# A two-layer transformer block on one core: idle matrix time filled, loads reordered, and a fixed instruction order taken from a plan

**Chip and metric.** One Trainium2 chip, one of its cores. Times are device microseconds of one execution. Traces and their views are in recorded spans of an execution. Most executions agree within half a per cent.

Names: PE is TensorE (matmul), DVE is VectorE, ACT is ScalarE, POOL is GpSimd, SP is SyncE.

## The reference

The input is one sequence of 2048 rows of 512 in bf16. A dilated local attention (32 heads of 16, every row looks at itself and 7 rows behind it, 2 apart) and a gated ReLU network, each behind a LayerNorm and added to its input:

```python
q, k, v = split(layernorm(x) @ wqkv)            # 512 x 1536
logits  = einsum("bhsd,bhswd->bhsw", q, k[idx]) * scale   # idx = pos - 2*w, w = 0..7, masked below 0
o       = einsum("bhsw,bhswd->bhsd", softmax(logits), v[idx])
h       = x + o @ wo
up, gate = layernorm(h) @ W_up, layernorm(h) @ W_gate     # 512 x 1376
h2      = h + ((gate * (gate > 0)) * up) @ W_down
```

## The kernel before

The rows go in four chunks of 512. Each step (a normalisation, a projection, a score product, a head sum) is an `Op` with an engine, an assumed duration and its inputs. A small planner simulates the engines while the program is built and so decides the order in which each engine gets its instructions; the hardware then runs each engine's list as it stands. `RANK` is a list of one number per operation. In the kernel before it is a priority only: the planner looks at everything that could start now and takes the best rank among it.

```python
LOOK = {"PE": 0.05, "DVE": 0.3, "ACT": 0.1}
def order(self):
    waiting = list(self.ops)
    while waiting:
        best = {}
        for op in waiting:                      # all operations whose inputs are done
            ...                                 # t = when inputs, engine and buffers allow it
            best.setdefault(op.eng, []).append((t, op))
        for eng, cands in best.items():
            first = min(t for t, _ in cands)
            t, op = min(((t, op) for t, op in cands if t <= first + self.LOOK.get(eng, 0.02)),
                        key=lambda x: (x[1].prio, x[1].seq))
        ...
```

What the planner assumes of the loads, and the loads themselves (x of chunk 0, then q, k and v weights, then the other x, then the big weights):

```python
xload = [[load(t) for t in (3.4, 3.5, 3.9, 3.9)]] + [[load(t)] * BPC for t in (9.7, 11.2, 12.7)]
wload = {n: load(t) for n, t in (("q", 6.3), ("k", 7.0), ("v", 8.3), ("o", 14.0), ...)}
...
for c, q in enumerate((nc.sync, nc.scalar, nc.sync)):
    q.dma_start(w3_sb[c][:], w3_r[:, :, c * D:(c + 1) * D])
for tk in range(1, NCK):
    nc.sync.dma_start(x_sm[:, tk * BPC:(tk + 1) * BPC, :], x_rows[:, tk * BPC:(tk + 1) * BPC, :])
```

The normalised rows of chunk 3 are transposed by SP's DMA queue and not by PE, and the first add of a head's eight weighted values is done by an accumulating DMA of POOL for the heads in `DACC`:

```python
DMAT = (("h",2,0),("h",2,2),("x",3,0),("x",3,2))
nc.sync.dma_start_transpose(out=dst.t[:, :, j * P:(j + 1) * P], in_=xn.t[:])
...
DACC = tuple((k, t) for k in range(3) for t in range(4))
nc.gpsimd.dma_start(mt.t[:, 0:4, :], mt.t[:, 4:8, :], accum_op=ALU.add)
```

The softmax here doesn't subtract the row's maximum and nothing guards it: scores larger than these inputs give would overflow.

Of the kernel before, what the change touches and what calls it, by code (L numbers as in the profile page):

```python
# [8 lines left out]
P = 128  # L9
# [8 lines left out]
RANK = [  # L18
    1, 3, 5, 2, 0, 4, 54, 6, 7, 30, 160, 197, 186, 250, 712, 8, 11, 10, 12, 14,
    17, 23, 27, 32, 20, 26, 31, 16, 18, 21, 24, 28, 33, 37, 9, 13, 15, 19, 22, 25,  # L20
    29, 34, 35, 65, 71, 68, 70, 73, 38, 60, 66, 56, 63, 69, 51, 61, 43, 55, 40, 50,
    45, 58, 83, 145, 79, 154, 76, 162, 74, 99, 80, 86, 96, 104, 110, 75, 67, 85, 89, 90,
    171, 179, 185, 114, 136, 123, 133, 128, 94, 113, 101, 108, 118, 148, 159, 183, 189, 193, 156, 170,
    199, 203, 205, 165, 176, 201, 204, 207, 142, 152, 181, 187, 192, 211, 218, 210, 215, 214, 222, 209,
    212, 227, 234, 221, 225, 228, 232, 226, 231, 239, 241, 246, 256, 249, 257, 261, 244, 259, 251, 260,
    264, 292, 321, 277, 317, 267, 313, 324, 333, 340, 280, 305, 270, 304, 301, 308, 303, 310, 315, 295,
    325, 307, 328, 285, 323, 319, 329, 335, 327, 344, 297, 341, 331, 346, 314, 339, 349, 350, 366, 343,
    358, 338, 365, 355, 372, 392, 334, 359, 348, 362, 397, 401, 421, 691, 717, 393, 407, 694, 718, 357,
    420, 701, 721, 363, 423, 699, 720, 39, 47, 44, 48, 36, 41, 42, 46, 49, 52, 62, 78, 64,
    77, 82, 57, 81, 59, 72, 84, 144, 191, 124, 188, 91, 178, 102, 182, 88, 164, 109, 169, 143,  # L30
    172, 117, 168, 147, 252, 139, 300, 87, 299, 151, 302, 195, 174, 224, 245, 229, 208, 238, 248, 253,
    258, 268, 273, 271, 284, 293, 296, 294, 290, 275, 283, 286, 287, 289, 298, 309, 345, 352, 318, 330,
    361, 367, 326, 337, 364, 368, 306, 316, 347, 351, 373, 378, 379, 386, 376, 382, 383, 395, 385, 389,
    391, 396, 390, 394, 398, 400, 402, 403, 406, 413, 408, 415, 419, 411, 417, 412, 418, 422, 431, 456,
    427, 454, 433, 460, 426, 452, 494, 439, 469, 441, 471, 434, 462, 436, 463, 500, 438, 466, 437, 465,
    479, 488, 464, 474, 503, 487, 496, 484, 491, 489, 498, 493, 501, 507, 450, 518, 458, 517, 506, 523,
    499, 520, 526, 447, 508, 444, 509, 524, 516, 536, 709, 726, 510, 530, 707, 725, 522, 538, 705, 723,
    533, 537, 703, 722, 98, 105, 92, 97, 93, 103, 53, 95, 112, 116, 126, 132, 125, 130, 146, 131,
    137, 129, 135, 150, 167, 216, 177, 217, 184, 220, 194, 223, 161, 240, 157, 237, 163, 242, 153, 213,
    173, 428, 175, 409, 202, 416, 219, 356, 236, 254, 265, 312, 274, 263, 288, 320, 322, 332, 336, 342,  # L40
    360, 353, 377, 375, 369, 374, 371, 384, 387, 381, 380, 430, 435, 453, 459, 414, 429, 446, 449, 424,
    432, 451, 457, 399, 425, 443, 448, 467, 473, 461, 468, 475, 482, 470, 478, 477, 480, 472, 476, 485,
    486, 481, 483, 490, 495, 519, 521, 511, 513, 528, 531, 497, 502, 543, 559, 540, 558, 549, 568, 548,
    565, 573, 560, 585, 567, 582, 575, 588, 544, 561, 594, 556, 578, 583, 593, 554, 576, 579, 590, 596,
    552, 570, 563, 580, 546, 564, 553, 574, 591, 616, 625, 572, 618, 599, 621, 608, 623, 631, 620, 630,
    587, 628, 633, 626, 642, 715, 731, 612, 639, 713, 729, 597, 635, 711, 727, 600, 640, 714, 730, 100,
    106, 115, 121, 111, 119, 107, 120, 122, 127, 140, 149, 155, 166, 134, 141, 138, 158, 247, 281, 180,
    255, 196, 269, 190, 266, 243, 279, 235, 278, 200, 272, 230, 276, 233, 541, 198, 505, 262, 550, 206,
    545, 291, 282, 311, 404, 370, 354, 388, 405, 410, 440, 442, 492, 445, 504, 529, 534, 527, 532, 455,
    525, 514, 515, 512, 542, 562, 581, 586, 535, 539, 555, 569, 551, 557, 566, 571, 547, 577, 584, 589,  # L50
    595, 603, 604, 611, 598, 607, 592, 601, 606, 609, 614, 615, 610, 613, 602, 605, 617, 619, 622, 624,
    636, 637, 641, 627, 634, 629, 632, 638, 646, 660, 650, 663, 647, 661, 644, 656, 675, 667, 677, 665,
    674, 673, 681, 670, 678, 684, 659, 671, 654, 668, 657, 669, 662, 672, 682, 651, 664, 652, 666, 643,
    655, 645, 658, 679, 683, 695, 648, 686, 680, 693, 649, 689, 697, 653, 688, 676, 690, 696, 685, 706,
    728, 736, 692, 700, 716, 732, 687, 702, 719, 734, 698, 704, 724, 735, 708, 710, 733, 737,
# [36 lines left out]
class Plan:  # L92
# [21 lines left out]
    GUIDE = ()  # L114

    def order(self):
        for kx, cx, ky, cy in self.GUIDE:
            xs = [o for o in self.ops if o.key and o.key[0].startswith(kx) and o.key[1] == cx]
            for o in self.ops:
                if o.key and o.key[0].startswith(ky) and o.key[1] == cy:  # L120
                    o.deps += xs
        waiting = list(self.ops)
        free = {}
        while waiting:
            best = {}
            for op in waiting:
                t = free.get(op.eng, 0.0)
                ok = True
                for d in op.deps:
                    if d.done is None:  # L130
                        ok = False
                        break
                    r = d.done + (self.HOP if d.eng != op.eng else 0.0)
                    if r > t:
                        t = r
                if not ok:
                    continue
                need = {}
                for b in op.take:
                    if b.i is None:  # L140
                        n = need[b.slots] = need.get(b.slots, 0) + 1
                        r = sorted(b.slots.free)[n - 1]
                        if r == float("inf"):
                            ok = False
                            break
                        t = max(t, r + self.HOP)
                if not ok:
                    continue
                best.setdefault(op.eng, []).append((t, op))
# [10 lines left out]
            t, op = pick  # L160
# [11 lines left out]
            waiting.remove(op)  # L172
# [4 lines left out]
def kernel(  # L177
# [88 lines left out]
    def setup():  # L266
# [4 lines left out]
        for c, q in enumerate((nc.sync, nc.scalar, nc.sync)):  # L271
            q.dma_start(w3_sb[c][:], w3_r[:, :, c * D:(c + 1) * D])
        for tk in range(1, NCK):
            nc.sync.dma_start(x_sm[:, tk * BPC:(tk + 1) * BPC, :], x_rows[:, tk * BPC:(tk + 1) * BPC, :])

        nc.sync.dma_start(wo_sb[:], A_wo.rearrange("(p t) f -> p t f", t=NT))
        nc.sync.dma_start(wu_sb[:], B_W_up.rearrange("(dt p) f -> p dt f", p=P))
        nc.sync.dma_start(wg_sb[:], B_W_gate.rearrange("(dt p) f -> p dt f", p=P))
        nc.sync.dma_start(
            wd_sb[:, 0:NFF, :], B_W_down[0:NFF * P, :].rearrange("(ft p) n -> p ft n", p=P))  # L280
        if FTAIL:
            nc.sync.dma_start(wd_sb[:FTAIL, NFF, :], B_W_down[NFF * P:F, :])

# [10 lines left out]
        nc.gpsimd.memset(vT[:, :, 0:PADL], 0.0)  # L294

# [20 lines left out]
    DACC = tuple((k, t) for k in range(3) for t in range(4))  # L316
    DAL = 5.5
    TDD, TDL = 2.4, 1.6
    NWARM = 48
    DMAT = (("h",2,0),("h",2,2),("x",3,0),("x",3,2))  # L320
# [8 lines left out]

    LNA = ((0, 0, 0, 0), (0, 0, 0, 0))  # L330
# [5 lines left out]
    A5, A10, AX, AS = 0.52, 0.92, 0.8, 0.2  # L336
# [4 lines left out]
    def load(t):  # L341
        return add(None, "LD", 0.0, None, lat=t)

    xload = [[load(t) for t in (3.4, 3.5, 3.9, 3.9)]] + [[load(t)] * BPC for t in (9.7, 11.2, 12.7)]
    wload = {n: load(t) for n, t in
             (("q", 6.3), ("k", 7.0), ("v", 8.3), ("o", 14.0), ("u", 18.0), ("g", 22.0), ("d", 27.0))}

    def layernorm(tk, src, dst_slots, pr, groups, on_act, residual=None):
# [7 lines left out]
        for grp in groups:  # L356
# [3 lines left out]
            for j in grp:  # L360
# [17 lines left out]
                elif tk == 0 and j == BPC - 1:  # L378
# [15 lines left out]
                    a = add(("xsu", tk), "ACT", 0.75, f_su, [src[j]], pr, take=[xns[j], sm], lat=AL)  # L394
                    a = add(("xnm", tk), "DVE", DSM, f_nm, [a], pr, take=[mv], use=[sm], lat=DL)
                    ag.append(add(("xsq", tk), "ACT", 0.75, f_sq, [a], pr, use=[mv, xns[j]], lat=AL))
# [51 lines left out]
            for j0 in range(lo, hi, step):  # L448
# [10 lines left out]
                for j in range(j0, min(j0 + step, hi)):  # L459
# [8 lines left out]
                    ds.append(add((ln + "tp" + gk, tk), "PE", 4 * TP, f_tp, [a], pr, take=[tp], use=[xn], lat=PEL))  # L468
                n = len(ds)
# [15 lines left out]
    wb = Buf(bank_s)  # L485

    def f_warm(wb=wb):
        for _ in range(NWARM):
            nc.tensor.matmul(wb.t[:, 0:P], lhsT=warm[:], rhs=warm[:], start=True, stop=True)

    add(("warm", 0), "PE", 5.2, f_warm, [], -500, take=[wb])

    kdone = {}
    for tk in range(NCK):
# [225 lines left out]
        hnT, hev = layernorm(tk, hd, hnT_s, base + 52, [[0, 1, 2, 3]], LNA[1][tk], residual=sm)  # L720
# [120 lines left out]
```

## Time and profile before

| | before |
|---|---|
| time, median of 3 | 203.58 us (203.55 to 204.13) |
| span of the profiled execution | 203.6 us, its own time 205.38 us |
| busy: PE, DVE, ACT, POOL | 96%, 76%, 63%, 6% |
| mean granted clock of that execution | 0.983 |

The lines of the profile are in the prediction.

### The profile page before, as it was taken

Reading aid. Unit: us, or ns where it says so; the run is one execution under the profiler, and the core shown is the slowest. Engines: PE = TensorE matmul, PEld = TensorE weight load, DVE = VectorE, ACT = ScalarE, POOL = GpSimd, SP = SyncE. Lnnn points to the kernel's source line nnn. Section 1 sums busy time; section 2 is a strip of 40 time slices with the busy share of each in tenths; the row PEclk is TensorE's granted clock in tenths of the full one; section 3 lists DMA queues with packets and bytes.
Section 4 is the critical chain, followed back from the end, with each engine's and each line's share of the span. In section 5 each row is a group of like instructions: output and inputs, shape, how many; then the busy total and the mean of one; then the engine's idle time right before and its main releaser. Section 6 shows DMA issues by size and latency. Waiting matters only on the chain.

```text
span 203.6 us, 2957 instructions
## 1 busy us (share of the span) xinstructions
PE 195.4 (96%) x1102; PEld 96.8 (48%) x1123; DVE 155.1 (76%) x246; ACT 127.7 (63%) x253; POOL 12.6 (6%) x26
## 2 busy tenths in 40 slices
PE   8499999999999999999999999999999999999994
PEld 8347545555545334444454444444444445444452
DVE  6549999999999999999999966599996255021314
ACT  3517879986569993797756599703665353576400
POOL 3000000330000002400033000000000000000000
PEclk9859999999999999999999999999999999999999
DMA  5999901698000002980059900400011001100003
GB/s 187 350 379 403 322 19 30 123 203 163 3 0 0 0 3 52 192 168 0 3 103 180 209 31 0 90 13 0 3 41 62 0 0 53 53 0 0 0 3 103
DMA packets 14893, 18.04 MB, mean 89 GB/s; under 512 B 5056, under 2 KB 12192, under 8 KB 14880
## 3 DMA queue, kind: packets, MB, share of 16 engines
q1 hardware_dynamic: 12336, 10.78, 16.4%
q0 software_dynamic: 1728, 6.29, 16.3%
q10 hardware_dynamic: 816, 0.79, 1.1%
q8 instruction: 9, 0.15, 0.3%
q14 instruction: 4, 0.03, 0.0%
HBM read 8.42 MB, written 2.10 MB: 52 GB/s over the span
## 4 chain that ended last, share of the span: by engine, by line
PE 93%; DMA 4%; issue 1%; SPq 0%; DVE 0%
PE bank L736 38%; PE bank L511 22%; PE bank L773 19%; PE bank L698 7%; DMA wq_sb<-in_A_wqkv_dram 4%; PE bank L564 4%; PE bank L465 2%; PE bank L625 1%; PE bank L597 1%; SPq L270 0%; DVE row L784 0%
## 5 line engine op out<-in xcount | busy, mean ns | idle before, releaser
L736 PE MATMUL bank<-quad,wg_sb 128*128 128x512 bf16 (+1 forms) x171 | 42.3, 379 | 0.3
L736 PE MATMUL bank<-quad,wu_sb 128*128 128x512 bf16 (+1 forms) x173 | 42.3, 379 | 0.1
L743 ACT ACTIVATE gr<-bank 128x512 bf16<-128x512 f32 (+1 forms) x44 | 26.0, 604 | 23.7 <-PE bank L736 18.3
L773 PE MATMUL bank<-wd_sb,gT 128*128 128x512 bf16 (+3 forms) x184 | 39.7, 366 | 0.2
L558 DVE TENSOR_TENSOR big<-quad,kT 128x4096 bf16<-128x4096 bf16 x16 | 36.0, 2284 | 0.1
L646 DVE TENSOR_TENSOR big<-big,vT 128x4096 bf16<-128x4096 bf16 x16 | 35.8, 2283 | 0.3 <-ACT big L631 0.3
L740 ACT CAST up_sb<-bank 128x512 bf16<-128x512 f32 (+1 forms) x44 | 25.7, 594 | 12.3 <-PE bank L736 8.5
L756 DVE TENSOR_TENSOR gT<-gr,up_sb 128x1024 bf16<-128x1024 bf16 (+1 forms) x24 | 15.4, 643 | 20.4 <-ACT gr L743 14.1
L773 PEld LDWEIGHTS <-gT 128*128 128x128 bf16 (+1 forms) x187 | 18.0, 98 | 19.3 <-issue 0.4
L736 PEld LDWEIGHTS <-wu_sb 128*128 128x128 bf16 (+1 forms) x176 | 17.3, 100 | 20.7 <-issue 1.3
L736 PEld LDWEIGHTS <-wg_sb 128*128 128x128 bf16 (+1 forms) x176 | 17.3, 100 | 20.6 <-issue 1.1
L511 PE MATMUL bank<-quad,wq_sb 128*128 128x512 bf16 (+1 forms) x70 | 16.9, 382 | 2.5 <-DMA wq_sb<-in_A_wqkv_dram 2.1
L631 ACT CAST big<-bank 128x512 bf16<-128x512 f32 x32 | 17.2, 610 | 1.5 <-PE bank L625 1.3
L511 PE MATMUL bank<-quad,wk_sb 128*128 128x512 bf16 (+1 forms) x70 | 16.8, 373 | 0.1
L678 POOL DMA_DIRECT2D big<-big x12 | 10.7, 894 | 98.3 <-DVE big L646 95.2
L784 DVE TENSOR_TENSOR row<-x_sm,bank 128x512 bf16<-128x512 bf16 (+1 forms) x17 | 10.6, 652 | 7.8 <-PE bank L773 7.8
L649 DVE TENSOR_TENSOR big<-big 128x1024 bf16<-128x1024 bf16 (+2 forms) x24 | 16.4, 727 | 0.0
L709 DVE SCALAR_TENSOR_TENSOR x_sm<-x_sm,bank 128x512 bf16<-128x512 bf16 x16 | 10.9, 685 | 6.8 <-PE bank L698 6.7
L511 PE MATMUL bank<-quad,wv_sb 128*128 128x512 bf16 x62 | 15.4, 379 | 0.1
L698 PE MATMUL bank<-wo_sb,quad 128*128 128x512 bf16 x61 | 14.8, 379 | 0.2
L371 ACT ACTIVATE row<-x_sm,mv 128x512 bf16<-128x512 bf16 x16 | 11.5, 717 | 4.5 <-DVE mv L363 4.4
L519 ACT CAST quad<-bank 128x512 bf16<-128x512 f32 x16 | 9.6, 601 | 7.4 <-PE bank L511 7.4
(65 smaller groups left out, 161.7 us busy)
## 6 DMA issues: line engine op xcount, KB each, us to landing
big<-big POOLq DMA_DIRECT2D x12, 512.0 KB, 5.5
out_dram<-row SPq DMA_DIRECT2D x15, 128.0 KB, 1.7
x_sm<-in_A_x_dram SPq DMA_DIRECT2D x3, 512.0 KB, 11.0
wu_sb<-in_B_W_up_dram SPq DMA_DIRECT2D x1, 1376.0 KB, 10.6
wg_sb<-in_B_W_gate_dram SPq DMA_DIRECT2D x1, 1376.0 KB, 13.9
wd_sb<-in_B_W_down_dram SPq DMA_DIRECT2D x1, 1280.0 KB, 15.7
wq_sb<-in_A_wqkv_dram SPq DMA_DIRECT2D x1, 512.0 KB, 8.4
wk_sb<-in_A_wqkv_dram ACTq DMA_DIRECT2D x1, 512.0 KB, 8.6
```

The costliest lines, as they stand in the source:

```text
L371: nc.scalar.activation(out=xn.t[:], in_=h.t[:] if h else x_sm[:, tk * BPC + j, :], func=ACT.Square, bias=mv.t[:, j, 0:1], scale=1.0, accum ...
L511: nc.tensor.matmul(mm.t[:, lo:hi], lhsT=w3_sb[c][:, dt, t:D:NT], rhs=xnT.t[:, dt, lo:hi], start=(dt == 0), stop=(dt == NT - 1))
L558: V.tensor_tensor(out=pb.t[:].rearrange("p (t w) s -> p t w s", t=2), in0=q4, in1=k4, op=ALU.mult)
L631: nc.scalar.copy(out=ab.t[:, w, :], in_=bc.t[:])
L646: V.tensor_tensor(out=mt.t[:], in0=ab.t[:], in1=v8, op=ALU.mult)
L649: V.tensor_tensor(out=mt.t[:, 0:n, :], in0=mt.t[:, 0:n, :], in1=mt.t[:, n:2 * n, :], op=ALU.add)
L698: nc.tensor.matmul(od.t[:], lhsT=OT.t[:, t, j * P:(j + 1) * P], rhs=wo_sb[:, t, :], start=(t == 0), stop=(t == NT - 1 and tk not in RPE))
L736: nc.tensor.matmul(mm.t[:fs, :], lhsT=w_sb[:, dt, ft * P: ft * P + fs], rhs=hnT.t[:, dt, :], start=(dt == 0), stop=(dt == NT - 1))
L740: nc.scalar.copy(out=ub.t[:fs, i, :], in_=um.t[:fs, :])
L743: nc.scalar.activation(out=gr.t[:fs, i, :], in_=gm.t[:fs, :], func=ACT.Relu)
L756: V.tensor_tensor(out=gt.t[:fs, 0:n, :], in0=gr.t[:fs, 0:n, :], in1=ub.t[:fs, 0:n, :], op=ALU.mult)
L773: nc.tensor.matmul(od.t[:, c0:c1], lhsT=gts[ft].t[:fs, ft % 2, j * P:(j + 1) * P], rhs=wd_sb[:fs, ft, c0:c1], start=(ft == 0), stop=(ft == ...
```

## The change

In the texts below, wo is the output projection, and a landing is the moment at which a transfer's completion is recorded.

The change's intent: get PE to work sooner and without loss of clock, and give every engine the order that a simulation found best. Five parts: (a) lots of nine matmuls on zeros behind the first transposes, (b) q weights split over two queues and ahead of the other loads, k behind a one-element copy that waits for x, (c) two of the twelve accumulating adds moved to DVE, (d) x of chunk 1 ahead of the v weights, (e) a new `RANK`, now a strict order for each engine, with new assumed times. In the plan a transpose by DMA is done at its start plus both numbers of `TDD, TDL`.

```diff
-    DACC = tuple((k, t) for k in range(3) for t in range(4))
+    DACC = tuple((k, t) for k in range(3) for t in range(4) if k or t < 2)
-    TDD, TDL = 2.4, 1.6
-    NWARM = 48
+    TDD, TDL = 1.25, 1.3
+    NWARM, NFILL = 48, 9
@@ order
+        if RANK:
+            queues = {e: [] for e in ("PE", "DVE", "ACT", "SP", "LD", "POOL")}
+            for op in sorted(waiting, key=lambda o: (o.prio, o.seq), reverse=True):
+                queues[op.eng].append(op)
-            for op in waiting:
+            for op in ([q[-1] for q in queues.values() if q] if queues else waiting):
@@ loads
-        for c, q in enumerate((nc.sync, nc.scalar, nc.sync)):
-            q.dma_start(w3_sb[c][:], w3_r[:, :, c * D:(c + 1) * D])
-        for tk in range(1, NCK):
+        for dt, q in ((0, nc.sync), (2, nc.scalar)):
+            q.dma_start(w3_sb[0][:, dt:dt + 2, :], w3_r[:, dt:dt + 2, 0:D])
+        ...
+        nc.gpsimd.tensor_copy(out=w3_sb[1][0:1, 0, 0:1], in_=x_sm[0:1, 0, 0:1])
+        for c, tk in ((1, 1), (2, 2)):
+            nc.sync.dma_start(w3_sb[c][:], w3_r[:, :, c * D:(c + 1) * D])
+            nc.sync.dma_start(x_sm[:, tk * BPC:(tk + 1) * BPC, :], x_rows[:, tk * BPC:(tk + 1) * BPC, :])
+        for tk in range(3, NCK):
             nc.sync.dma_start(x_sm[:, tk * BPC:(tk + 1) * BPC, :], x_rows[:, tk * BPC:(tk + 1) * BPC, :])
@@ assumed landings
-    ... for t in (9.7, 11.2, 12.7)]      ("q", 6.3), ("k", 7.0), ("v", 8.3)
+    ... for t in (9.3, 12.4, 14.0)]      ("q", 6.3), ("k", 7.7), ("v", 10.8)
@@ behind each transpose of chunk 0
+            for _ in range(NFILL):
+                nc.tensor.matmul(wb.t[:, 0:P], lhsT=warm[:], rhs=warm[:], start=True, stop=True)
```

Not in the diff: the numbers of `RANK`, some assumed durations, the split of one group of transposes, and four edges for the planner.

## The prediction

> **What bounds the kernel now.** I read the page first, then the chain that ended last in order of time, then TensorE's (PE's) own stretch by stretch listing, then the first 20 us in windows of 1 us, then VectorE's (DVE's) listing. The page says that PE is the bound:
>
> ```profile
> PE 195.4 (96%) x1102; PEld 96.8 (48%) x1123; DVE 155.1 (76%) x246; ACT 127.7 (63%) x253; POOL 12.6 (6%) x26
> PE   8499999999999999999999999999999999999994
> DVE  6549999999999999999999966599996255021314
> PEclk9859999999999999999999999999999999999999
> PE 93%; DMA 4%; issue 1%; SPq 0%; DVE 0%
> ```
>
> The reader is to see two things. PE is full in every slice except the second and the last, so only the start and the tail can be shortened. And in the third slice (10.2 to 15.3 us) PE is full but its granted clock is half. DVE is also full from slice 5 to slice 22 (about 15 to 112 us), which matters below. The chain of waits at its start:
>
> ```profile
> 1.66 8.42 DMA wq_sb<-in_A_wqkv_dram
> 10.08 0.05 issue
> 10.13 2.32 PE bank L511 x9
> ...
> 200.66 0.02 issue
> 200.69 0.42 DVE row L784
> ```
>
> The first projection starts at 10.13 us, when the q weights land; PE then runs without a gap to 200.66, and 2.9 us of last addition and output follow. So time = start of first projection + 190.5 + 2.9. In windows of 1 us (the columns are window, length, PE, PEld, DVE, ACT, POOL, clock, DMA share, GB/s):
>
> ```profile
> 8.00:9.00 1.00, 0.05 (x1) 0.00 (x0) 0.26 (x1) 0.61 (x2) 0.00 (x0) 0.90 0.96 310
> 9.00:10.00 1.00, 0.00 (x0) 0.00 (x0) 0.00 (x0) 0.00 (x0) 0.00 (x0) 0.50 1.09 382
> 12.00:13.00 1.00, 0.78 (x3) 0.29 (x2) 0.00 (x0) 0.00 (x0) 0.00 (x0) 0.50 1.13 366
> 15.00:16.00 1.00, 1.00 (x5) 0.38 (x3) 1.00 (x6) 0.53 (x1) 0.00 (x0) 0.69 1.05 402
> 16.00:17.00 1.00, 1.00 (x7) 0.51 (x5) 1.00 (x2) 0.56 (x3) 0.00 (x0) 1.00 1.01 392
> ```
>
> The clock is halved from about 8.8 to 15.6 us. The order of instructions has 8 matmuls of 256 columns and 16 of 512 between 10.13 and 17.16 us. Later in the trace a 512-column matmul takes 0.216 us (four in 0.864), so these should take 8 x 0.108 + 16 x 0.216 = 4.3 us; they took 7.0. **Lost to the clock: 2.7 us.**
>
> DVE, the second-tightest engine (start, duration, line, operation, idle before):
>
> ```profile
> 13.20 1.29 DVE L401 BATCH_NORM_STATS2 st<-x_sm 128x6 f32<-128x512 bf16 x2 [4.94 <-DMA x_sm<-in_A_x_dram]
> 17.55 1.39 DVE L436 TENSOR_SCALAR row<-x_sm,mv,rs 128x512 bf16<-128x512 bf16 x4 [0.42 <-ACT rs L418]
> 18.84 8.90 DVE L558 TENSOR_TENSOR big<-quad,kT 128x4096 bf16<-128x4096 bf16 x4
> 52.43 0.75 DVE L653 TENSOR_TENSOR quad<-big,rec 128x512 bf16<-128x512 bf16 x2
> 93.39 0.75 DVE L672 TENSOR_TENSOR quad<-big 128x512 bf16<-128x512 bf16 x2
> ```
>
> x of chunk 1 lands at 13.2, DVE does its statistics, starts the first score product at 18.84 and is gapless from there. Its last scaling of chunk 0 ends at 53.1 (PE's output projection wo of chunk 0 starts at 54.33), its last head sum of chunk 1 at 94.1 (PE's wo of chunk 1 at 94.40). So behind PE there stands a DVE chain with only 1.2 and 0.3 us of slack. That is the point on which my prediction turns.
>
> **What the Trainium skill says.** "TensorE: Matmul & The Clock Gate", Part 1: the array clock is at half rate by default, and a free-running window of some 3.4 us of activity releases or restores it. The trace agrees: the half-rate stretch is 15.6 - 8.8 = 6.8 us, two such windows, after a stretch in which PE worked only about 2 of 3.4 us. "DMA: Bandwidth & Descriptors", Issuing engines are not separate DMA queues: transfers started by different engines run on the same 16 DMA engines and interleave. Agrees: q and k weights, issued together at 1.66 on two queues, land at 10.1 and 10.3 though 1.57 MB (x of chunk 0, q, k) had been moved by about 7 us at the rates of the windows. The same page, Why a DMA increments its semaphore by 16 and not by 1: a transfer counts as landed only when the slowest of its engines is done. The trace shows such a tail: DMA share falls to 0.21 at 25 to 26 us, and the last big load lands at 28.1. TensorE's page, Architectural detail: ACT and DVE are strict FIFO and PE may only pull weight loads ahead. So an order fixed beforehand waits where it is wrong; this trace, with PE never waiting after 10.1, cannot show the cost.
>
> **The change part by part.**
> (a) *Fillers.* Four lots of nine 128-column matmuls follow the transposes of chunk 0. At 0.056 us (16 transposes in 0.89 us later in the trace) a lot is 0.5 us. In the built order two lots come after the second transpose and before the third, one in the middle of chunk 0's projections, one just before the first score sum. The first two keep the clock up: gain 2.7 us, cost little. The other two are on PE's path: +1.0 us.
> (b) *q weights first.* Split over two queues; k waits for the first x block to land (3.4), a one-element POOL copy and the issue, so it starts to move near 4.7. x of chunk 0 plus q is 1.05 MB, moved by about 5.4 us; q should land at 6 to 8 and stops being the bound. Then the transposes are: in the before trace group 0's exponential waits at 5.99 behind a Square of 0.7 us; a new order edge lets it go at about 5.4. Normalising two rows 5.8 to 6.5, transposes to 6.9, 18 fillers to 7.9, two more transposes to 8.4, and only then the first projection. **Start 8.4 instead of 10.13: -1.7 us.**
> PE alone would thus give 203.6 - 1.7 - 2.7 + 1.0 = **200.2 us**. That is a floor: PE work after it is unchanged.
> (c) *Chunk 0's last two heads* lose the accumulating DMA and get the add on DVE: 2 x 1.14 us (2048-element adds back to back) = +2.3 us on DVE.
> (d) *x of chunk 1 ahead of v weights; x of chunk 2 stays fifth.* Before, the fourth 0.5 MB block (v) landed at 11.7, the fifth (x1) at 13.2, x2 at about 14.6 (3.6 + 11.0). If a place in the row keeps its landing time, x1 now lands near 11.7 and x2 near 14.6. If the gate really thins the row out, x1 about 9.5 and x2 about 12.5.
> (e) *Strict order.* DVE must now do three of chunk 2's four statistics before the first score product, so that product starts at D = x2 landing + 2 statistics (1.2) + four normalisations (1.35), one more statistic (0.6) and small ones: x2 + 3.5. That is 16.0 (x2 at 12.5) to 18.1 (x2 at 14.6), against 18.84.
> From D to the end: DVE to the last scaling of chunk 0 took 34.3 before; now one product less (-2.2), one statistic less (-0.6), two adds more (+2.3): 33.7. PE then has everything from wo of chunk 0 on: 146.3 before, and the order moves three groups of four 512-column matmuls behind it (+2.6) with a few small pieces saved: 148.6. Later, chunk 1's broadcast waits for a scaling that my sum of DVE's instructions puts some 0.8 us behind PE. Tail 2.9, hop 0.1. Sum: 33.7 + 0.1 + 148.6 + 0.8 + 2.9 = **D + 186.1**, against D + 184.8 before. With D = 16.0: 202.1; with 17.0: 203.1; with 18.1: 204.2.
>
> **The rivals.**
> 1. *PE stays the bound.* Then 200.2, or 199.8 if the transposes come earlier. For it: the before trace has no PE wait after 10.1. Against it: PE would come to wo of chunk 0 at 8.4 + 39.9 = 48.3, six us earlier than now, and DVE could only follow if D were 14.7, that is x2 landed by 11.2.
> 2. *DVE's chain takes the wait over* (my main case), 201.5 to 204.2: the start gained on PE is given back in waits at the first score sum (near 20 to 22 us) and at wo of chunk 0.
> 3. *k's weights become the new wait.* They come second in PE's order, after only 0.43 us of q work, and as third block might land at 10 as before. PE would idle about 1.2 us there, and the clock might drop again. Alone: 201.4; under rival 2 mostly hidden.
> 4. *The strict order goes wrong* (an eviction of ACT behind a logarithm that waits for x1's statistics, a buffer returned late): ACT's is there at position 15 of its order. Each such step costs 1 to 3 us, up to 206.
>
> **Range and chances.** The four changes at the start are worth 3.4 us net to PE, and I expect somewhat over half of that to be eaten by DVE's chain. I put x2 nearer to the thinner row, since q, k and x1 no longer compete with everything, and take 202.2. Low end 200.3 is the PE floor; high end 204.3 is x2 at its old time. Faster by over 2% means below 199.5, under the floor: 0.08. Slower by over 2% means above 207.6, and needs several bad waits: 0.03.
>
> **What would show it.** Right: clock 1.0 throughout from 5.5 us; first projection near 8.4; the first waits of PE after it being for DVE score products and the head scaling of chunk 0, some 1 to 3 us in sum; PE work after wo of chunk 0 about 148.6. Wrong: no PE wait after the first projection (then about 200); k or v weights as the longest PE wait (rival 3); half clock somewhere in 8 to 20 us (fillers too few); or long waits late, beyond 100 us (rival 4).

## The result

The changed kernel takes **208.87 us** (208.12 to 209.34, 4 runs) against 203.56 us in the same rounds: ratio 1.0254 (1.0216 to 1.0293), slower by over 2%. Ratios here are the mean time of one kernel's fast runs over that of the other's of the same rounds, so not quite the ratio of the medians quoted. Executions over 1.5% slower than the fastest of the same kernel are left out of the means.

The page after (engines' busy shares; PE and granted clock in 40 slices; the chain's shares by engine):

```profile
PE 195.8 (94%) x1140; PEld 98.9 (48%) x1159; DVE 157.9 (76%) x248; ACT 125.1 (60%) x255; POOL 10.8 (5%) x25
PE   8699889699999899999999999999999999999991
PEclk9999999999999999999999999999999999999999
PE 76%; DVE 8%; DMA 8%; SPq 2%; issue 2%; ACT 1%; POOL 0%
```

The clock is full throughout, as intended. But PE, which before had no hole after its first projection, now has some (slices 5, 6, 8 and 14, besides the second), and DVE, DMA and SP stand on the chain. PE's waits (what it waited for: us in all, times, longest):

```profile
PE bank L542 <- DMA quad<-row: 1.9, 1, 1.9
PE bank L542 <- DMA wk_sb<-in_A_wqkv_dram: 1.5, 1, 1.5
PE bank L656 <- DVE ex L614: 1.0, 2, 0.6
PE bank L595 <- DVE big L589: 0.5, 1, 0.5
PE bank L656 <- DVE ex L643: 0.4, 1, 0.4
```

They sum to 5.3 us. The chain of waits in time (start, length, what) shows where the longest comes from: x of chunk 2, the products and norms of DVE, then four transposes by SP's queue, one after the other, the last of which takes 5.2 us to land (the three ahead of it take 2.4 to 2.5):

```profile
5.15 9.54 DMA x_sm<-in_A_x_dram
...
18.10 4.38 DVE big L589 x2
...
34.60 1.26 SPq L490
...
35.95 5.23 DMA quad<-row
...
41.31 3.40 PE bank L542 x15
...
203.39 0.42 DVE row L815
```

PE's and DVE's listings at the places that answer to those of before (start, length, instruction, idle before it):

```profile
8.25 0.60 PE L542 MATMUL bank<-quad,wq_sb 128*128 128x256 bf16 x4
53.83 3.62 PE L729 MATMUL bank<-wo_sb,quad 128*128 128x512 bf16 x15
```

```profile
11.70 1.88 DVE L437 BATCH_NORM_STATS2 st<-x_sm 128x6 f32<-128x512 bf16 x3 [3.05 <-DMA x_sm<-in_A_x_dram]
18.02 4.46 DVE L589 TENSOR_TENSOR big<-quad,kT 128x4096 bf16<-128x4096 bf16 x2
50.97 0.76 DVE L684 TENSOR_TENSOR quad<-big,rec 128x512 bf16<-128x512 bf16 x2 [1.23 <-ACT rec L634]
```

PE starts its first projection 1.9 us sooner than in the profile of before. Yet wo of chunk 0 starts at 53.83 instead of 54.33: nearly all of the start is lost by then. DVE waits 1.23 us for a reciprocal of ACT. The sum that it needs stands in PE's fixed order behind the first projections that waited for the transposes, and in ACT's own fixed order the reciprocal (50.29) comes behind six evictions of further projections, each late by that wait.

Why the fourth transpose is slow: POOL issued the first accumulating transfer at 35.84, SP the transpose at 35.95, and they landed at 41.00 and 41.17. Run 14 below bears on that. Had the transpose taken 2.5 us like the others, it would have landed at about 38.5 (an estimate from these figures), before PE came to need it at 39.4; PE's longest wait would not have been there.

A ledger follows for the changed kernel and the first three runs (the mended kernels' is further down). Take the start of the last row's addition, subtract the start of the first projection, PE's waits after it as its listing flags them, and 1.0 us where two lots of fillers stand on PE's path. What is left is PE's own work.

| kernel | first projection | PE's waits | fillers on path | own work | last addition to end |
|---|---|---|---|---|---|
| changed | 8.25 | 5.29 | 1.0 | 188.9 | 4.1 |
| before + fillers | 9.82 | 0.52 | 0 | 189.0 | 2.8 |
| before + new loads | 8.08 | 1.21 | 0 | 188.5 | 3.3 |
| before + both | 9.78 | 0.19 | 0 | 189.0 | 3.3 |

PE's own work agrees within 0.6 us (runs 6, 8 and 9 give 188.8 to 189.0). So PE is the bound in all of them, and **each wait of PE goes into the time in full**. The changed kernel wins 1.9 us at the start against a start at 10.1, and pays 5.3 us of waits, 1.0 us of fillers and about 1.2 us at the end: 5.6 us, as the spans show (207.5 against 201.9, the mean span of 37 executions of the kernel before; a span is 1.9 us shorter than its time, on average over them). The kernel before would add up to nearly that without any wait: 10.1 + 188.7 + 2.9 = 201.7. That last sum is not shown, though: the start at 10.1 is that of the one profile, an uncommon execution, whose own work is 187.9 us once the 2.7 us of half clock are taken off; and with the same loads q landed at 8.51 and 8.87 us in two other profiles (runs 1 and 6). The timed executions may start earlier and wait later.

### The profile page after: what moved, and what is told of

It reads as the page before. It is cut to its first block, busy times and chain, and to the rows that moved or that the text cites. A ratio compares the mean times of both kernels' runs of the same rounds, so it can differ in the third digit from the quotient of the medians.

```text
span 207.5 us, 3017 instructions
## 1 busy us (share of the span) xinstructions
PE 195.8 (94%) x1140; PEld 98.9 (48%) x1159; DVE 157.9 (76%) x248; ACT 125.1 (60%) x255; POOL 10.8 (5%) x25
## 4 chain that ended last, share of the span: by engine, by line
PE 76%; DVE 8%; DMA 8%; SPq 2%; issue 2%; ACT 1%; POOL 0%
PE bank L767 36%; PE bank L804 18%; PE bank L542 10%; PE bank L729 7%; DMA x_sm<-in_A_x_dram 6%; DVE big L589 4%; DMA quad<-row 3%; PE bank L595 2%; DVE st L437 2%; DVE row L472 2%; PE bank L501 1%; SPq L490 1%; PE bank L628 1%; ACT big L662 1%; PE bank L656 1%
## 5 line engine op out<-in xcount | busy, mean ns | idle before, releaser
L771 ACT CAST up_sb<-bank 128x512 bf16<-128x512 f32 (+1 forms) x44 | 24.9, 586 | 28.0 <-PE bank L767 25.5
L804 PE MATMUL bank<-wd_sb,gT 128*128 128x512 bf16 (+2 forms) x182 | 39.3, 366 | 0.3
L774 ACT ACTIVATE gr<-bank 128x512 bf16<-128x512 f32 (+1 forms) x44 | 25.3, 604 | 11.3 <-PE bank L767 10.4
L680 DVE TENSOR_TENSOR big<-big 128x1024 bf16<-128x1024 bf16 (+2 forms) x26 | 19.2, 768 | 0.1
L542 PE MATMUL bank<-quad,wq_sb 128*128 128x512 bf16 (+1 forms) x71 | 16.3, 356 | 1.9 <-DMA quad<-row 1.9
L542 PE MATMUL bank<-quad,wk_sb 128*128 128x512 bf16 (+1 forms) x68 | 15.5, 355 | 1.6 <-DMA wk_sb<-in_A_wqkv_dram 1.5
L517 ACT COPY quad<-bank 128x1024 bf16<-128x1024 bf16 (+1 forms) x12 | 11.1, 946 | 6.7 <-PE bank L501 6.7
L709 POOL DMA_DIRECT2D big<-big x10 | 8.8, 877 | 102.8 <-DVE big L677 102.8
```

Source lines behind the costliest of these rows:

```text
L542: nc.tensor.matmul(mm.t[:, lo:hi], lhsT=w3_sb[c][:, dt, t:D:NT], rhs=xnT.t[:, dt, lo:hi], start=(dt == 0), stop=(dt == NT - 1))
L680: V.tensor_tensor(out=mt.t[:, 0:n, :], in0=mt.t[:, 0:n, :], in1=mt.t[:, n:2 * n, :], op=ALU.add)
L771: nc.scalar.copy(out=ub.t[:fs, i, :], in_=um.t[:fs, :])
L774: nc.scalar.activation(out=gr.t[:fs, i, :], in_=gm.t[:fs, :], func=ACT.Relu)
L804: nc.tensor.matmul(od.t[:, c0:c1], lhsT=gts[ft].t[:fs, ft % 2, j * P:(j + 1) * P], rhs=wd_sb[:fs, ft, c0:c1], start=(ft == 0), stop=(ft == ...
```

## The experiments

All fourteen gave correct results. Each was timed beside the kernel before, whose median was 203.55 to 204.11 us. "The changed kernel" is 1.0254 on its own chip; other lots ran on other chips, and it was not timed again beside them, so ratios are compared, not times.

### 1 to 4: parts alone, and the fixed order

**Fillers alone**, with the order of the kernel before untouched:

```diff
 transposes of block j of chunk 0 (kernel before)
+  for _ in range({1: 9, 2: 30}.get(j, 0)):
+      nc.tensor.matmul(wb.t[:, 0:P], lhsT=warm[:], rhs=warm[:], start=True, stop=True)
```

> The kernel before with 39 filler matmuls behind its transposes of chunk 0 (9 after the second, 30 after the fourth), order of everything else untouched, loads untouched. Theory A (behind PE stands a VectorE chain with about 0.3 us of slack, which starts with the landing of x of chunk 1 at 13.2 us): the clock is full from 8 to 16 us, yet the time falls by at most 0.5 us, and PE shows new waits for VectorE's products instead. Rival (PE alone is the bound, as its unbroken row says): about 2.7 us less than the profiled run before, that is some 200.9 to 202.7 us. If the half clock of the run before was only chance of that run, both say about 203.

Measured: 204.37 us, ratio 1.0022 (0.9996 to 1.0048), clock 1.0 in the profile. The 2.7 us do not come. The profile says why in three ways. The fillers themselves hold the first projection up: q landed at 8.51 us, the last transposes of chunk 0 end at 8.31, yet the first projection starts at 9.82, behind 30 fillers (smaller lots were not tried in this order). A wait for DVE's product has appeared, and DVE in turn waits for an accumulating transfer:

```profile
PE bank L568 <- DVE big L562: 0.5, 1, 0.5
```

```profile
50.45 1.36 DVE L653 TENSOR_TENSOR big<-big 128x1024 bf16<-128x1024 bf16 x3 [0.91 <-DMA big<-big]
```

And the runs of the kernel before beside it show that there was little to win: of 37 such executions 29 had a clock of 0.998 or more (mean 203.69 us) and 8 one of 0.989 to 0.992 (mean 203.96 us). None had the 0.983 of the profile that I had read, which took 205.38 us.

**New loads alone** (parts b and d of the diff, in the kernel before):

> The kernel before with the new order of loads alone (q weights split over two queues, k behind a gate, x of chunk 1 ahead of v weights, x of chunk 2 after v). Theory A: loads are not what made the changed kernel slower; q lands near 7, k near 10.2, x of chunk 1 near 11.7, the first score product at 17.3 instead of 18.84, and the time falls by 0.5 to 1.5 us. Rival (the new order of loads is what hurts: k weights alone late, v late): 204.5 or more, with PE waiting for k and v weights 1.5 us or more in sum.

Measured: 202.91 us, ratio 0.9951 (0.992 to 0.9983). The first projection starts at 8.08, x of chunk 1 lands at 10.91, the first score product starts at 16.37 and no weight load is waited for. The rival falls. Theory A's 0.5 to 1.5 us are met (1.2 us between the medians). PE's waits are for DVE:

```profile
PE bank L471 <- DVE row L442: 1.1, 2, 0.7
PE bank L570 <- DVE big L564: 0.5, 1, 0.5
```

**Both:**

> Both together: fillers and loads, in the order of the kernel before. Theory A: 201 to 202.5 us, because PE starts earlier at full clock and VectorE's chain starts 1.5 us earlier too; so the two gains that the change was to bring are real, and the new fixed order is what loses them. Rival (the loads or the fillers hurt): 204 or more.

Measured: 204.35 us, ratio 1.0018. Theory A's 201 to 202.5 is missed. With q early, the 30 fillers end at about 9.8 and hold the first projection up: it starts at 9.78 instead of 8.08. So fillers in that number cost 1.7 us, nearly what the 30 last (1.84), as soon as nothing else is waited for. This run still tells that neither loads nor fillers make the 5 us: with the order of before they cost 0.2% in all.

**The changed kernel, ranks as priorities:**

```diff
-        if RANK:
+        if False:
             queues = {...}
-    ... for t in (9.3, 12.4, 14.0)]      ("q", 6.3), ("k", 7.7), ("v", 10.8)
+    ... for t in (11.7, 14.7, 16.1)]     ("q", 6.7), ("k", 10.2), ("v", 13.2)
```

> The changed kernel with its list of ranks used as priorities only (the look-ahead planner of the kernel before picks what can start), and the measured landing times of the loads in the plan instead of the assumed ones. Theory A (the fixed order is the loss, built on landing times 2.4 us too early for x and 4 us too early for the transposes by DMA): 202 to 205 us, that is 4 to 7 us less than the changed kernel's 208.9. Rival (other parts of the change lose the time: two head sums moved to VectorE, loads, fillers): 207.5 to 209.

Measured: 212.11 us, ratio 1.0376 (1.0328 to 1.0424); three of the four runs have a clock of 0.992, the one at full clock took 210.72. A clear miss, for the rival too. The list was made for strict use, and the look-ahead planner makes other mistakes with it:

```profile
PE bank L767 <- ACT quad L517: 3.0, 2, 1.6
PE bank L542 <- DMA quad<-row: 2.9, 1, 2.9
```

So taking the strictness away, with this list, mends nothing (the run changes the assumed landings too, and tries no other list, so it does not clear strictness as such). The next runs look for particular places in the list.

### 5 to 8: one part of the change undone at a time

**Chunk 3's projections later** in the fixed order (name.chunk; q0 to q11 are the twelve projection groups of a chunk):

```diff
 PE order ahead of wo of chunk 0 (ACT's evictions likewise)
-q3.2 q0.3 q6.2 q2.2 q7.3 den.0 q7.2 q10.2 q10.1 q10.3 q8.1 q4.3 q11.2 q2.3 q9.2 q6.3
+q3.2 q6.2 q2.2 den.0 q7.2 q10.2 q10.1 q8.1 q11.2 q9.2 q0.3 q7.3 q10.3 q4.3 q2.3 q6.3
```

> The changed kernel with six groups of chunk 3's projections, and their evictions, moved behind nine groups of chunks 1 and 2 in the fixed order (what comes before wo of chunk 0 stays the same work). PE then needs the fourth transpose by DMA, which landed at 41.17 us, only near 46. Theory A (that wait of 1.88 us, with VectorE's wait of 1.23 us for the reciprocal that it causes, is on the path): 206.5 to 207.3 us against 208.9. Rival (some other wait ends at the same time and takes its place, or VectorE's chain alone sets wo of chunk 0): 208.4 or more.

Measured: 206.33 us, ratio 1.0136 (1.0096 to 1.0176): 1.2% of the 2.5% are gone, some 2.4 us. The profile has no wait for the transposes any more, nor DVE one for the reciprocal; wo of chunk 0 starts 33.8 us behind the first score product instead of 35.8. The fourth transpose still took 5.2 us, only nobody waited for it. (The profile fell on a run with early loads, so k was not waited for either; its span is 3.7 us less than the changed kernel's, more than the 2.4.)

```profile
PE bank L656 <- DVE ex L614: 1.0, 2, 0.6
PE bank L656 <- DVE ex L643: 0.4, 1, 0.4
PE bank L595 <- DVE big L589: 0.4, 1, 0.4
```

**Loads of before in the changed kernel** (parts b and d undone):

> The changed kernel with the loads of the kernel before (q and k together, v, then x of chunks 1 and 2). Theory A (PE waited for k until 10.3 us in the changed kernel anyway, and VectorE's first product hangs on x of chunk 2, whose landing the new order of loads left at 14.7): 208.4 to 209.4, nothing lost, since nothing had been gained. Rival (the earlier start of PE and of x of chunk 1 is worth something in the changed kernel): 210.2 or more.

Measured: 209.53 us, ratio 1.0315 (1.0259 to 1.0371), with one run at 211.49, whose clock is 0.992. Just above theory A's band and below the rival's: the new loads are worth 0 to 1% in the changed kernel, and are not its loss.

**Without the four filler lots**, order untouched:

```diff
-            for _ in range(NFILL):
+            for _ in range(0):
```

> The changed kernel without the four lots of nine fillers (order of the rest untouched, the 48 first ones stay). Theory A (two of the lots stand on PE's path but right before waits, for k and for a score product, which then grow by as much): 208.4 to 209.2. Rival 1 (fillers cost what they last): about 207.9. Rival 2 (without them the clock falls to half between 8 and 16 us and that counts): 210 or more with a clock of 0.985 or less.

Measured: 209.72 us, ratio 1.0276 (1.02 to 1.0353). Mixed: two runs at a clock of 0.998 or more took 208.05 and 208.53 us, a run at 0.991 took 210.91 and one at 0.992 took 211.61. The last is the one profiled, and it shows where its half clock lies (windows as in the prediction):

```profile
8.00:16.00 8.00, 6.20 (x48) 4.86 (x48) 4.42 (x11) 2.67 (x7) 0.00 (x0) 1.00 1.05 359
44.00:45.00 1.00, 1.00 (x4) 0.39 (x3) 1.00 (x3) 0.00 (x0) 0.00 (x0) 0.50 0.36 66
```

From 8 to 16 us, where the fillers were to keep it up, the clock is full without them. It is halved from 43.1 to 46.5 us, behind PE's wait of 2.25 us for the fourth transpose; in run 4's profile, with all fillers in, it is halved from 44.5 to 47.9, behind a wait of 2.90 us for the same. So no profile here shows that the fillers are what keeps the clock up, and rival 2's mechanism is not seen. Where the clock stays up without them, they cost well under 1 us. They are not the loss.

**All twelve accumulating DMAs:**

```diff
-    DACC = tuple((k, t) for k in range(3) for t in range(4) if k or t < 2)
+    DACC = tuple((k, t) for k in range(3) for t in range(4))
```

> The changed kernel with the two adds of chunk 0's last heads back on the accumulating DMA (12 instead of 10). Theory A (PE is held by the transposes and by its place in the fixed order, and two more transfers of 512 KB crowd the transposes further): 208.3 to 209.8. Rival (the 2.3 us of adds on VectorE ahead of wo of chunk 0 are the loss): 206.4 to 207.

Measured: 210.13 us, ratio 1.0345 (1.0281 to 1.041): no gain, so the rival falls; it is rather slower than the change (1.0254), though the intervals overlap. In the fixed order DVE's next add stands right behind the transfer and waits for it:

```profile
47.08 0.69 DVE L680 TENSOR_TENSOR big<-big 128x1024 bf16<-128x1024 bf16 x1 [5.68 <-DMA big<-big]
```

That run therefore does not tell what the adds cost on DVE; run 14 does.

### 9 to 12: mending the named places

**The end.** In the changed kernel SP's second last-chunk store waits for DVE's fourth addition, and three stores stand behind it; SP issues them until 204.96 us, though the last addition ends at 203.81:

```profile
197.73 7.23 SPq L819 DMA_DIRECT2D out_dram<-row  x6
```

```diff
 DVE's last additions (rows)   and SP's last stores
-2 0 3 1 4                     -3 1 2 0 4
+3 2 0 1 4                     +3 2 0 1 4
```

> The changed kernel with only the last five additions of VectorE and the last five stores reordered so that both follow the order in which PE ends the rows (in the fixed order the second of the stores waits for the fourth addition, and three others stand behind it). Theory A (that is the 0.8 us by which the time from the last addition to the end grew, 2.9 to 3.7 us): 0.6 to 1.0 us less than the changed kernel, a ratio of about 1.021 to the kernel before. Rival (the longer end comes from the stores themselves, not from their order): no change, 1.025.

Measured: 207.91 us, ratio 1.0192 (1.016 to 1.0224). Start of the last addition to the end: 3.3 us instead of 4.1, which is the 0.8 expected. The ratio fell by 1.3 us' worth, more than that says; in its profile k was waited for 0.6 us less, too (0.85 instead of 1.46). The other 0.4 us over the 2.9 of before also stands in the kernel before with the new loads (3.3), so it comes with these; how is not shown.

**All mends together**, with both broadcasts of chunk 0 one projection group later and the two filler lots on the path emptied:

```diff
-... q9.0 fill sc1.0 q1.1 q4.1 bc1.0 q5.1 ...   bc0.0 q6.1
+... q9.0      sc1.0 q1.1 q4.1 q5.1 bc1.0 ...   q6.1 bc0.0
```

> The changed kernel with all that the traces name mended, and still with its fixed order, loads and fillers in front: chunk 3's six groups later, the end reordered, both broadcasts of chunk 0 one projection group later, the two filler lots on PE's path emptied. Theory A (waits of PE add up: 1.9 to 2.5 for the transposes, 0.8 for the end, 1.0 for the broadcasts, up to 1.0 for the fillers, of which VectorE's chain takes some back): 202.8 to 204.5 us, a ratio of 0.997 to 1.005. Rival (the fixed order costs in many more places than these): 205.5 or more.

Measured: 205.53 us, ratio 1.0104 (1.0065 to 1.0144). Above theory A's band in ratio and just on the rival's side in time: 1.5% of the 2.5% are accounted for, not all. PE's waits fell from 5.3 to 2.6 us, but one grew: as PE gets to the first score sum earlier, it waits longer for DVE.

```profile
21.07 0.61 PE L595 MATMUL bank<-big,sel 128*32 128x512 bf16 x8 [1.41 <-DVE big L589]
```

**The kernel before with new loads and a plan that knows them:**

```diff
-    ... for t in (9.7, 11.2, 12.7)]      ("q", 6.3), ("k", 7.0), ("v", 8.3)
+    ... for t in (10.9, 13.9, 15.4)]     ("q", 6.9), ("k", 9.8), ("v", 12.5)
```

> The kernel before with the new loads, and with the landing times of those loads as measured put into its plan, so that three groups of chunk 0's v projections go ahead of the first transposes of chunk 1. PE's wait of 0.68 us for x of chunk 1 should go. Theory A (VectorE's chain stands 0.3 us behind PE at wo of chunk 1): 0.2 to 0.6 us less than with the new loads alone, that is a ratio of 0.992 to 0.994. Rival (PE alone is the bound): 0.7 to 1.2 us less, 0.989 to 0.992.

Measured: 203.31 us, ratio 0.9966 (0.9937 to 0.9995), no better than new loads alone (0.9951). The wait of 0.68 us is gone, and PE waits 0.72 us for a DVE product at 63.8 us in its place. DVE's chain stands right behind PE; the rival falls, and theory A's gain of 0.2 to 0.6 us does not come either.

**PE's groups put into its waits:**

```diff
-sc1.0 q1.1 q4.1 q5.1 ...   wo.0 q8.2 q4.2
+q1.1 q4.1 sc1.0 q5.1 ...   q8.2 q4.2 wo.0
```

> The mended version of before, with two of chunk 1's projection groups put ahead of the first score sum, where PE still waited 1.41 us for VectorE's second product, and two of chunk 2's groups put ahead of wo of chunk 0 instead of behind it. Theory A (what is left, some 2 us, is the work that the fixed order put behind wo of chunk 0 while PE waited for VectorE ahead of it): 149.8 us from wo of chunk 0 to the last addition become about 148.1, wo of chunk 0 stays near 33.6 us behind the first score product, and the time is 203.4 to 204.4 us, a ratio of 0.997 to 1.002. Rival (the rest is lost elsewhere, or the first waits only move on to other places): 1.007 or more.

Measured: 206.76 us, ratio 1.0167 (1.0127 to 1.0207): theory A fails here. The wait of 1.41 us is gone, but the groups themselves wait for ACT, and from wo of chunk 0 to the last addition it is still 149.6 us, not the expected 148.1. As wo of chunk 0 starts later, DVE gets its sums later and, it seems, PE so waits for DVE further on. PE's waits are 3.5 us in all.

```profile
19.89 1.02 PE L542 MATMUL bank<-quad,wk_sb 128*128 128x512 bf16 x4 [0.78 <-ACT quad L517]
66.61 0.40 PE L656 MATMUL bank<-ex,spread 32*128 32x512 bf16 x4 [1.07 <-DVE ex L643]
```

### 13 and 14: the two adds on DVE

```diff
 run 13, on the mended changed kernel: DVE behind the four products of chunk 0
-add add add | product of chunk 1 | six small adds, scalings | product
+product of chunk 1 | heads 1, 3 | product | heads 0, 2        (all 12 adds by DMA)
 run 14, on the kernel before with new loads
-    DACC = tuple((k, t) for k in range(3) for t in range(4))
+    DACC = tuple((k, t) for k in range(3) for t in range(4) if k or t < 2)
```

> The mended changed kernel (chunk 3's groups later, end reordered, broadcasts later, no fillers on the path) with all 12 accumulating DMAs, and VectorE's order after the four products of chunk 0 as in the kernel before (one product of chunk 1, two heads' small adds, another product, the other two heads), so that no add waits for its transfer. Theory C (the rest of the loss is 2.3 us more of adds on VectorE, which both engines' later waits hand on): 1.2 to 2.2 us less than the mended one, a ratio of 0.999 to 1.004. Rival (the rest is the order of PE behind wo of chunk 0): no gain, 1.008 or more.

Measured: 205.47 us, ratio 1.0106 (1.0073 to 1.0139): no gain over the mended kernel (1.0104). Theory C fails there. DVE is free sooner and then waits for PE, while PE's wait at the score sum stays:

```profile
21.63 0.61 PE L595 MATMUL bank<-big,sel 128*32 128x512 bf16 x8 [1.42 <-DVE big L589]
```

```profile
51.74 0.69 DVE L740 SCALAR_TENSOR_TENSOR x_sm<-x_sm,bank 128x512 bf16<-128x512 bf16 x1 [1.10 <-PE bank L729]
```

> The kernel before with the new loads, and with the two accumulating DMAs of chunk 0's last heads put on VectorE as in the change. Theory C: VectorE's chain is the second bound with 1.0 us or less of slack at wo of chunk 0 and almost none at wo of chunk 1, so 1.0 to 2.3 us more than with the new loads alone, a ratio of 1.000 to 1.007. Rival (the adds are hidden): 0.5 us or less more, 0.995 to 0.998.

Measured: 205.17 us, ratio 1.008 (1.0047 to 1.0114), against 0.9951 without the two adds: 1.3%, some 2.6 us, a little over the band's upper end. In the order of before the adds are not hidden at all: PE's waits rise from 1.2 to 2.7 us, and wo of chunk 0 starts at 53.48 instead of 51.41.

This run shows one thing more, which it was not made for. With the two heads off the accumulating DMA, POOL issues the first such transfer at 37.22 us, 1.5 us behind the fourth transpose (35.69). In the fifteen other profiles the transfer was issued just ahead of that transpose (by at most 0.8 us), and the transpose landed right after it (by at most 0.7 us), 4.9 to 5.7 us from its issue. The landings of the eight transposes (least, median, most), in the kernel before and in this run:

```profile
DMA to landing us min/median/max: 2.4/2.5/5.4
DMA to landing us min/median/max: 2.4/2.5/2.8
```

So the slow fourth transpose goes with an accumulating transfer just ahead of it. In the changed kernel that is the longest wait of PE. A run made to test it, the changed kernel with that transfer held back, is missing.

The ledger for the mended kernels:

| kernel | first projection | PE's waits | fillers on path | own work | end | ratio |
|---|---|---|---|---|---|---|
| chunk 3 later | 8.30 | 1.85 | 1.0 | 188.5 | 4.1 | 1.0136 |
| all mends | 8.23 | 2.62 | 0 | 189.1 | 3.3 | 1.0104 |
| groups in the waits | 8.51 | 3.48 | 0 | 189.1 | 3.3 | 1.0167 |
| all mends, 12 DMAs | 8.37 | 2.77 | 0 | 189.1 | 3.3 | 1.0106 |
| before + loads + 2 adds | 8.10 | 2.73 | 0 | 189.0 | 3.3 | 1.0080 |
| before + loads, plan told | 8.09 | 1.20 | 0 | 188.4 | 3.3 | 0.9966 |

**What stays open.** The mended kernel is still 1.5% behind the kernel before with new loads (some 3 us; 2.1 in the profiles' spans, 203.2 against 201.1). Of the 2.1, 1.4 us are PE's waits and 0.6 us are "own work", whose spread I cannot explain. The waits are nearly all for DVE in each trial, but not at the same places; no single edit removed them. And run 13 and run 14 differ on whether the two adds matter, presumably because the two orders around them differ. I leave it at that: the rest may lie in how the two engines' lists fit each other; I could not name one instruction for it.

**Best version.** New loads alone in the kernel before: 202.91 us, 0.5% faster than the kernel before, with the whole interval (0.992 to 0.998) below 1.

## Why the prediction was wrong

Predicted 202.2 (200.3 to 204.3), measured 208.87. By its own steps:

- **Start 8.4:** right, 8.25. **Full clock:** right, 0.999. **Rival 3, k as a new wait of about 1.2 us:** happened in the profiled run (1.46) but not in every one: 0.7 to 1.8 us in three more profiles of the fixed order with the new loads, none in four.
- **"Lost to the clock: 2.7 us":** right for the trace that I read, wrong for the kernel. That execution took 205.38 us, the timed ones 203.6. I set its span (203.6) beside the median time (203.58) as if they were the same thing; a span is 1.9 us under its time. So that gain was counted from an uncommon execution; it enters the floor of 200.2, though, and not the D + 186.1 that gave 202.2. The whole sum, which is in spans, was handed in as a time: that is 1.9 us of the error. The clocks of the 37 timed executions show that there was little to give.
- **D, the first score product, "x2 + 3.5", 16.0 to 18.1, taken as 16.1:** the rule held (14.7 + 3.3 = 18.0; and 3.3 in all seven further profiles of the fixed order with the new loads), and of the two landing times offered, the unfavourable one came true: the sixth 0.5 MB block in the row (the prediction calls it the fifth) landed when the sixth had landed before. I chose the thinner row without a measurement for it. +1.9 us in the profiled execution; that is partly its bad luck, as in those seven profiles x of chunk 2 landed between 12.7 and 14.9 us.
- **"33.7" from D to wo of chunk 0 (33.8 with the hop):** measured 35.8. This is the step that failed in its mechanism. It summed DVE's instructions and took for granted that none waits. The fixed order put chunk 3's projections ahead of the work that DVE's last scalings need by way of ACT's reciprocal. They waited 1.9 us for the fourth transpose, and DVE then 1.2 us for the reciprocal. I had listed the transposes by DMA nowhere. Without that wait the term is 33.8 (run 5) and 33.6 (run 10), so the sum itself was right. +2.0 us.
- **"148.6 + 0.8" behind wo of chunk 0:** right, 149.6 from wo to the last addition.
- **"Tail 2.9":** 4.1. It was copied from before, and I did not compare the order of the last five stores. 0.8 us of the 1.2 is that order (run 9). +1.2 us.

The sum: 1.9 + 2.0 + 0.2 + 1.2 = 5.3, which leads from 202.2 to the profiled span of 207.5; and 1.8 more to its time of 209.34, which lay 0.5 above the median.

Rival 4, "the strict order goes wrong", is what happened in kind, and its upper end of 206 was in spans too; but neither the places that it names nor its sign, long waits beyond 100 us, came true: PE's last wait is at 68.9. The main case, rival 2, named waits at the first score sum, which came (0.5 us at 22.5), and at wo of chunk 0, which did not. Giving rival 4 almost no chance was the error of judgement: the change asked me to trust an order computed from assumed times, while the numbers to check them stood in the trace. The plan has x of chunk 1 at 9.3 (landed 11.7), x of chunk 2 at 12.4 (14.7), k at 7.7 (10.2). Each was too early. It has each transpose ready 1.25 + 1.3 = 2.55 us after its start, which is right for three of the four (2.4 to 2.5) and 2.7 us too early for the fourth, which went with the accumulating transfer that the plan kept apart from it by an edge and the chip did not. The trace of before shows it already: there the fourth took 5.4 us. That this wait became a loss is shown by run 5; what slows the transpose is a coincidence in fifteen profiles and its absence in one (run 14), not a test; for the loads the delays are measured, their share in the loss is only argued.

## What to carry to other kernels

When one engine is the bound and has no holes, an earlier start is worth nothing by itself: list what each neighbour must deliver earlier too, and count every new wait at full length. An order frozen from a plan is as good as the worst landing time assumed in it; check each assumed time against the trace, loads and transfers by other queues first, before trusting the order, and ask which steps the plan keeps apart that nothing on the chip keeps apart. And before a loss seen in a profile is counted as a gain to come, compare that execution's own time with the timed runs.

## What the Trainium skill lacked or had wrong

- "TensorE: Matmul & The Clock Gate", Part 1, describes the free-running window and what an idle one costs. The lengths agree with the traces (6.8 us, two windows, in the kernel before; 3.4 in runs 4 and 7). What set the half rate off agrees less: before none of these stretches was PE idle for a whole window. It had worked 1.9 of the 3.4 us before it in the kernel before (1.4 of them transposes), and in runs 4 and 7 the half rate followed waits of 2.90 and 2.25 us. The page gives no word on how often one and the same program falls back from run to run: the kernel before had next to no half rate in 29 of 37 executions and, reckoned from the clocks of 0.989 to 0.992, some 3 to 4.5 us of it in 8, while the first profile had 6.8 (0.983). In the 8 it was worth 0.3 us of time. Under the changed order it was worth more: of the fast runs, those at 0.991 or 0.992 took 1.6 to 2.6 us longer than the others of runs 4, 6 and 7, though not all of that need be the clock's, since in the two profiles the half rate follows a long wait.
- "DMA: Bandwidth & Descriptors", DMA Transpose (X-bar), has no duration for a 128x512 bf16 transpose between tiles of SBUF issued by SP. Here each holds SP's queue for 1.2 us; the landing takes 2.5 us at the median and 5.2 us at worst. The slow one was issued just behind an accumulating transfer (35.84, the transpose at 35.95), as in fifteen of sixteen profiles; in run 14, where that transfer came 1.5 us behind it, it landed in 2.5 us. No page says what a transpose loses just behind an accumulating transfer.
- The same page, Issuing engines are not separate DMA queues, says that transfers interleave, but nothing on how far a landing varies. x of chunk 1, the fourth 0.5 MB block in the same row of loads, landed between 9.7 and 12.0 us in thirteen profiles with the new loads, and, there the fifth, between 12.1 and 13.2 in three with the old ones; in these three the q weights landed between 8.5 and 10.1.
- No page has the time of an accumulating DMA of 512 KB within SBUF: 5.1 to 5.8 us at the median of each of the sixteen profiles, whereas the same add takes DVE 1.14 us.
